# Scores and head mixing of an attention kernel as 64 by 64 products in the quarters of the TensorE array

## Chip, cores and metric

The kernel runs on one core of one Trainium2 chip. The metric is the time of one execution in microseconds (us), as the device measures it; of several runs the median counts. Engines are named as in the profile: PE is the matrix engine (TensorE) and PEld its weight loads, DVE the vector engine, ACT the scalar engine, POOL GpSimd, SP the engine that issues most of the transfers. A chunk is a set of rows of the score matrix that goes through the softmax together.

## What is computed

Talking-heads attention for 8 batches, 12 heads, 448 positions and head dimension 64, followed by a feed-forward layer with a squared ReLU:

```
scores = 0.125 * q @ k^T                      # per batch and head: 448 x 448
scores = einsum('bhij,hg->bgij', scores, w_pre)    # mixes the heads
attn   = softmax(scores, over j)
attn   = einsum('bhij,hg->bgij', attn, w_post)     # mixes the heads again
x      = (attn @ v), heads side by side       # 3584 x 768
out    = relu(x @ w_in)**2 @ w_out            # 768 -> 2048 -> 768
```

Inputs and output are float32; the products run in bfloat16.

## The kernel before, in words

**Scores.** A batch has 448 query rows: 384 of them in three sets r = 1, 2, 3 of 128 rows (row 3p + r - 1 of partition p), and 64 rest rows as set r = 0. `score` (L681) multiplies queries by keys. For r > 0 the contraction is 64 long, so the two heads of a pair go into the upper and lower half of the array's rows: two products 64x128 by 448 columns, each into its own PSUM bank, which run together. This is the planner's mode ROWS. DVE or ACT copies each bank into `snat` (L487, L489).

**Relayout and mixing.** Head mixing needs all heads of a row on different partitions. `relayout` has SP issue a transfer (L709) that gathers 10 rows times 12 heads from `snat` into the 120 partitions of one of 11 buffers `sch`, partition = row * 12 + head. `chunk` then multiplies by `wmix` (L807), a 120x120 matrix which holds ten copies of the 12x12 matrix `w_pre` on its diagonal, scaled and negated: one product 120x128 by 448 columns on the full array. A batch has 45 chunks: 6 of r = 0 (C0 = [0, 6, 19, 32]) and 13 of each other r, the first of which gathers leftovers. In the first batch 14 chunks take another way (L813), which the change leaves alone.

**Softmax and second mixing.** DVE reduces the bank to the minimum (L818), ACT takes the exponential with a running sum (L821), DVE the reciprocal (L827), POOL scales `wback`, the second mixing matrix, by it (L830). Four PE products (L837) multiply the exponentials by that matrix; this mixes, normalizes and transposes at once. The result is copied to `atb`. When half a batch is there, `av` (L882) multiplies by the values: two heads in the two halves of the array's columns, mode COLS.

**Feed-forward.** For every two batches `unit` runs `w_in` (L941), ReLU on DVE or ACT, the square on POOL (L962) and `w_out` (L980), on 128 or 256 columns at a time. These products have the lowest priority and fill PE's gaps.

**The order** is fixed when the kernel is built. `Planner.run` plays all operations through with a cost for each (a mix 190 ns, a pair's scores 190, a change of mode TURN = 95) and records them in the order in which they started; the engines then work strictly in that order. Each operation has a priority, in chunk numbers, and its inputs. PE prefers to stay in a mode, for at most STAY chunk numbers past an operation of another mode that is ahead. PSUM has 8 banks: MOST limits mixes ("m") to 3 banks, scores and others ("g") to 6, and the attention kinds together ("mix") to 7. Where PE would stand idle early in the run, `stand` (L1191) puts in products of zeros.

Of the kernel before, what the change touches and what calls it, by code (L numbers as in the profile page):

```python
# [23 lines left out]
NJ = 3  # L24
# [5 lines left out]
KC = CI * H  # L30
C0 = [0, 6, 19, 32]
# [15 lines left out]
ROWS, COLS = 1, 2  # L47
# [5 lines left out]
STAY = {ROWS: 2, COLS: 6}  # L53
# [4 lines left out]
MOST = {"m": 3, "a": 2, "f": 2, "g": 6, "mix": 7}  # L58
# [29 lines left out]
class Op:  # L88
    def __init__(self, engs, lat, pri, fn, deps, bank, frees, mode):
        self.engs, self.lat, self.pri, self.fn = engs, lat, pri, fn  # L90
        self.bank = bank if isinstance(bank, list) else [bank] if bank is not None else []
        self.frees, self.mode = frees, mode
        self.rows = None
        self.left, self.next, self.at, self.eng, self.ns = 0, [], None, None, 0
        for d in deps:
            if d is not None:
                self.left += 1
                d.next.append(self)
# [23 lines left out]
class Planner:  # L122
# [18 lines left out]
    def run(self):  # L141
# [22 lines left out]
        t, mode, clock = 0, 0, Clock()  # L164
# [16 lines left out]
        while True:  # L181
            for eng, heap in ready.items():
# [23 lines left out]
                kept, short, first = [], False, None  # L206
                while heap:
                    item = heapq.heappop(heap)
                    op = item[2]
                    if op.eng is not None:  # L210
                        continue
                    wide = len(op.bank) > 1
                    if not fits(op) or (short and op.bank and op.bank[0][0] in HOLD):
                        short = short or wide
                        kept.append(item)
                        continue
                    if eng == "PE" and mode and op.mode != mode and first is None:
                        first = item
                        kept.append(item)
                        continue  # L220
                    if first is not None:
                        if op.mode != mode or op.pri > first[0] + STAY[mode]:
                            kept.append(item)
                            if op.pri > first[0] + STAY[mode]:
                                op, item = first[2], first
                                kept.remove(first)
                            else:
                                continue
                    args = []
                    break  # L230
                else:
                    item = None
                    if first is not None:
                        kept.remove(first)
                        item, op, args = first, first[2], []
                if item is None and eng == "PE" and free and IDLE_FROM <= t < IDLE_END and (
                    t < 9000 or clock.at(t) > 1 or clock.share(t - SPELL, t) < IDLE_LOW
                ):
                    op = Op({"PE": 0}, 0, 0, self.still, [], None, None, mode)
                    op.eng, op.ns, op.at = "PE", IDLE_NS * clock.at(t), t  # L240
                    clock.spells.append((t, t + op.ns))
                    order.append((op, [free[0], mode]))
                    busy[eng] = t + op.ns
                    heapq.heappush(events, (t + op.ns, n, None))
                    n += 1
                if item is not None:
# [7 lines left out]
                    op.eng, op.ns, op.at = eng, op.engs[eng], t  # L254
                    if eng == "PE":
                        op.ns = (op.ns + TURN * (op.mode != mode)) * clock.at(t)
                        clock.spells.append((t, t + op.ns))
                        mode = op.mode
# [45 lines left out]
def kernel(  # L304
# [30 lines left out]
    sch = many(NSCH, "sch", [KC, S], BF16)  # L335
    schl = sb.tile([KC, S], BF16, name="schl")
    es = many(NE, "es", [KC, S], BF16)
    mn = many(NE, "mn", [KC, 1], F32)
    sm = many(NE // 2, "sm", [KC, 2], F32)
    rc = many(NE // 2, "rc", [KC, 2], F32)  # L340
    wq = many(NE, "wq", [KC, H, CI], BF16)
# [49 lines left out]
    wpre_rep = sb.tile([KC, H], F32, name="wpre_rep")  # L391
    wpost_rep = sb.tile([KC, H], F32, name="wpost_rep")
    smask = sb.tile([KC, CI], F32, name="smask")
    wmix = many(3, "wmix", [KC, P], BF16)
    for t_ in wmix:
        nc.vector.memset(t_[:, KC:P], 0.0)
    wback = sb.tile([KC, H, CI], F32, name="wback")
    nmask = sb.tile([KC, CI], F32, name="nmask")
    perm = sb.tile([KC, KC], BF16, name="perm")

    own = sb.tile([KC, H], F32, name="own")
# [14 lines left out]
    def pick(to, of, mask):  # L416
        parts = hr[0][0:KC, 0:H * H].rearrange("p (g h) -> p g h", g=H)
        nc.vector.tensor_tensor(
            out=parts, in0=wall[0:KC, H * H * of:H * H * (of + 1)].rearrange("p (h g) -> p g h", g=H),
            in1=mask[:, :].unsqueeze(1).to_broadcast([KC, H, H]), op=ALU.mult,  # L420
        )
        nc.vector.tensor_reduce(out=to[:, :], in_=parts, axis=AX.X, op=ALU.add)

    def pick_near():
        nc.vector.tensor_reduce(
            out=own[:, :], in_=ident[0:KC, 0:KC].rearrange("p (s h) -> p h s", s=CI), axis=AX.X, op=ALU.add,
        )
        pick(wpre_rep, 0, own)
        pick(wpost_rep, 1, own)
# [23 lines left out]
    def near_masks():  # L453
        nc.vector.tensor_reduce(
            out=smask[:, :], in_=ident[0:KC, 0:KC].rearrange("p (s h) -> p s h", s=CI), axis=AX.X, op=ALU.add,
# [5 lines left out]
            out=perm[:, :].rearrange("k (s x p) -> k s x p", s=CI, x=2),  # L461
            in_=ident[0:KC, 0:KC].rearrange("k (s p x) -> k s x p", s=CI, x=2),
        )

    def near_mix():
        for t_ in wmix[1:]:
            nc.vector.tensor_tensor(
                out=t_[:, 0:KC].rearrange("p (s h) -> p s h", s=CI),
                in0=wpre_rep[:, :].unsqueeze(1).to_broadcast([KC, CI, H]),
                in1=nmask[:, :].unsqueeze(2).to_broadcast([KC, CI, H]), op=ALU.mult,  # L470
            )

    def near_back():
        nc.gpsimd.tensor_tensor(
            out=wback[:, :, :], in0=wpost_rep[:, :].unsqueeze(2).to_broadcast([KC, H, CI]),
            in1=smask[:, :].unsqueeze(1).to_broadcast([KC, H, CI]), op=ALU.mult,
# [188 lines left out]
    def groups(b, r):  # L665
        size = GROUP if b >= GROUP_AT and r > 0 else 1
        return [range(p, p + size) for p in range(0, NPAIR, size)]

    def score(b, r, group):
        sn = store_of(b, r)  # L670
        p = group[0]
        tag = "g"
        keys = [(tag, "s", b, r, p_, x) for p_ in group for x in range(1 if r == 0 else 2)]

        def mms(*got):
            for key, slot in zip(keys, got):
# [4 lines left out]
                nc.tensor.matmul(slot[:, 0:S], lhsT=lhsT, rhs=kt[i][half, :, at_, :], start=True, stop=True)  # L681
# [7 lines left out]
            "PE", 190 * len(group), pri, keep(keys, mms), ins + old, lat=200, bank=keys, mode=ROWS * (r > 0),  # L689
        )  # L690
        for p_ in group:
# [23 lines left out]
    def relayout(b, c):  # L715
# [8 lines left out]
        if r == 2 and cc == 0:  # L724
            src_of[n] = schl
            here.append(move(n, pri, 780, deps + side.get(b - 1, []), schl[24:96, :], sn[120:126, :, :], lat))
# [13 lines left out]
        else:  # L740
            parts = [(blk, 0, KC, sn[cc - 1:cc + CPR * (CI - 1):CPR, :, :])]
        for of, r0, r1, srcs in parts:
            ns = 860 if r1 - r0 > 90 else 590
            relay_of.setdefault(of, []).append(move(n, pri, ns, deps + old, src_of[n][r0:r1, :], srcs, lat))
        if r == 0 and cc == 5 and b > 0:
            here.append(move(
                place_of(b, C0[2]), pri + 0.5, 500, deps + side.get(b - 1, []),
                schl[0:24, :], sn[124:P, 0:NPAIR, :], lat,
# [17 lines left out]

    def chunk(b, c):
        n = place_of(b, c)
        r, cc = block_of(c)
        rows = 96 if c == C0[2 if b else NJ] else KC  # L770
        ns = rows // H
        far = is_direct(b, c)
        src = None if far else src_of[n]
        wm = wmix[0 if r == 0 else 2 if cc == 0 and r < NJ else 1]
        back = wback_far if far else wback
# [50 lines left out]
        def f_rc():  # L826
            nc.vector.reciprocal(out=rc[i // 2][:, :], in_=sm[i // 2][:, :])  # L827
# [16 lines left out]
        def f_ac(eng):  # L844
# [6 lines left out]
        m = m_op[n] = add(  # L851
            "PE", mix_ns, n, keep(mk, f_m),
            relay.get(n, []) + [at_op.get(n - NE), w_ready if not far else None] + mix_deps, lat=200, bank=mk,
# [4 lines left out]
        e = exp_op[n] = add("ACT", 626, n + 0.4, f_exp, [x, at_op.get(n - NE), rc_op.get(n - NE)], lat=190, frees=mk)  # L858
        if n % 2 == 0:
# [5 lines left out]
        w = wq_op[n] = add("POOL", 370, n + 0.5, f_wq, [s_, at_op.get(n - NE)] + (backed_far if far else backed), lat=70)  # L865
# [147 lines left out]
    def pieces(pair, pos, part=None):  # L1013
        e0, e1 = (0, DMODEL) if part is None else part
        got = []
        for bb in range(2):
            row = (2 * pair + bb) * S
            for j, first in enumerate(PLACES[bb]):
# [9 lines left out]
                view = out[row:row + CPR * CI * NJ, :].rearrange("(s c r) e -> r c s e", c=CPR, r=NJ)  # L1028
# [24 lines left out]
    def w_turn(slot):  # L1053
        nc.tensor.matmul(
            slot[0:KC, 0:KC], lhsT=perm[:, :], rhs=wmix[1][:, 0:KC], start=True, stop=True,
        )

    def w_put():
        for t_, hi in ((wmix[0], KC), (wmix[2], 24)):
            nc.vector.tensor_copy(out=t_[0:hi, 0:KC], in_=slots["m", "w"][0:hi, 0:KC])  # L1060
# [6 lines left out]
    backed.append(add("POOL", 420, NEAR_AT, near_back, [fetched, masked]))  # L1067
    w_ready = add(
        "DVE", 300, NEAR_AT, w_put, [add("PE", 200, NEAR_AT, keep(("m", "w"), w_turn), [mixed], lat=200, bank=("m", "w"))], frees=("m", "w"),
    )  # L1070

# [74 lines left out]
    def next_batch(b):  # L1146
# [11 lines left out]
        for r in range(NJ + 1):  # L1158
            for p in groups(b, r):
                score(b, r, p)  # L1160
            for c in range(C0[r], (C0 + [NCHUNK])[r + 1]):
                relayout(b, c)
# [26 lines left out]
    def stand(slot, mode):  # L1189
        k_, m_ = P // 2 if mode == ROWS else P, P // 2 if mode == COLS else P  # L1190
# [41 lines left out]
```

## Time and profile before

| what | value |
|---|---|
| median of 3 runs | 579.14 us (579.02 to 579.38) |
| the profiled execution | 577.99 us |
| its span, first to last instruction | 576.2 us |
| granted PE clock, mean | 0.999 |
| mixes L807 on PE | 346 products (339 of `sch` recorded on one row, 7 of `schl` on another) |
| scores L681 on PE in row halves | 276 products |
| value transposes L837 | 1440 products |
| feed-forward L941, L980 | 1632 and 912 products |
| reduces L818, exponentials L821 | 360 each |

The table's counts are from the groups of the profile, which list source line, engine, operation, tiles, shapes and count, then the busy time and the mean duration of one, then the engine's idle time just before and what ended it. The mean duration of a PE product (354 ns for 448 columns) runs from its start to the end of its last column's way through the array. Products that follow each other overlap there, so the pace is read from start to start, on the timeline. "128*128" on a PE row are the rows and columns of the array that the product takes. The timeline gives start and length in us, and merges equal instructions that follow each other ("x4").

### The profile page before, as it was taken

How to read it: one execution, taken by the hardware profiler on the slowest of the kernel's cores; microseconds unless marked ns; L12 is line 12 of the kernel's file. 1: busy time of each engine (PE TensorE's matmuls, PEld its weight loads, DVE VectorE, ACT ScalarE, POOL GpSimd, SP SyncE). 2: the span in 40 equal slices, each digit the busy share in tenths (PEclk: the TensorE clock that was granted, in tenths of full speed). 3: DMA queues.
4: the chain of work that ended last, by engine and by line, in shares of the span. 5: the costliest groups of instructions: out<-in, count | busy, mean ns of one | idle time of the engine just before them, and what ended most of it. 6: DMA issues, size and time to landing. Idle time of an engine off the chain costs nothing.

```text
span 576.2 us, 16829 instructions
## 1 busy us (share of the span) xinstructions
PE 565.1 (98%) x5830; PEld 407.5 (71%) x5830; DVE 510.2 (89%) x1124; ACT 445.9 (77%) x1185; POOL 329.4 (57%) x609
## 2 busy tenths in 40 slices
PE   8999999999999999999999999999999999999997
PEld 5668766786776767677667677777758676767784
DVE  7999998999999999989899988999799898989442
ACT  5798988878778887988888988888888888888100
POOL 8267445764575548646567357845767444735341
PEclk9999999999999999999999999999999999999999
DMA  9999849963898639963697638984497646322021
GB/s 135 211 182 224 158 116 208 163 151 87 132 202 156 159 100 184 173 151 111 137 181 148 164 104 144 188 152 139 109 205 158 147 121 117 124 81 75 1 56 55
DMA packets 131678, 80.79 MB, mean 140 GB/s; under 512 B 59286, under 2 KB 126600, under 8 KB 131592
## 3 DMA queue, kind: packets, MB, share of 16 engines
q1 hardware_dynamic: 84760, 56.88, 40.3%
q0 software_dynamic: 46784, 22.81, 30.8%
q8 instruction: 45, 0.74, 0.6%
q14 instruction: 41, 0.34, 0.2%
q10 hardware_dynamic: 48, 0.02, 0.0%
HBM read 45.61 MB, written 11.01 MB: 98 GB/s over the span
## 4 chain that ended last, share of the span: by engine, by line
PE 87%; DVE 6%; DMA 3%; ACT 2%; issue 1%; POOL 0%; DVEq 0%; ACTq 0%; POOLq 0%
PE bank L980 24%; PE bank L941 23%; PE bank L837 12%; PE bank L807 11%; PE bank L882 7%; PE bank L681 6%; DMA sch<-snat 3%; PE bank L813 2%; DVE mn L818 1%; DVE atb L487 1%; DVE snat L487 1%; PE bank L1191 1%; ACT es L821 1%; DVE qn L612 1%; ACT snat L489 0%
## 5 line engine op out<-in xcount | busy, mean ns | idle before, releaser
L821 ACT ACTIVATE es<-bank,mn 120x448 bf16<-120x448 f32 x360 | 228.5, 643 | 37.0 <-DVE mn L818 32.6
L818 DVE TENSOR_REDUCE mn<-bank 120x1 f32<-120x448 f32 x360 | 209.7, 611 | 1.2 <-PE bank L807 1.1
L830 POOL TENSOR_SCALAR wq<-wback,rc 120x120 bf16<-120x120 f32 (+1 forms) x346 | 123.0, 367 | 148.4 <-DVE rc L827 90.3
L980 PE MATMUL bank<-w,h 128*128 128x384 bf16 (+2 forms) x912 | 184.1, 323 | 0.0
L941 PE MATMUL bank<-xt,w 128*128 128x256 bf16 (+1 forms) x1632 | 164.7, 254 | 0.3 <-ACT hr L959 0.2
L962 POOL TENSOR_TENSOR h<-hr 128x512 bf16<-128x512 f32 x112 | 116.4, 1041 | 64.8 <-DVE hr L955 34.9
L941 PEld LDWEIGHTS <-w 128*128 128x128 bf16 x1632 | 136.1, 98 | 22.8 <-issue 2.4
L837 PEld LDWEIGHTS <-es 120*112 120x112 bf16 (+1 forms) x1440 | 110.9, 129 | 27.7 <-ACT es L821 3.7
L837 PE MATMUL bank<-wq,es 120*112 120x120 bf16 (+1 forms) x1440 | 120.8, 217 | 0.5 <-ACT es L821 0.2
L980 PEld LDWEIGHTS <-h 128*128 128x128 bf16 x912 | 83.7, 98 | 51.7 <-issue 5.2
L487 DVE CAST atb<-bank 112x480 bf16<-112x480 f32 (+3 forms) x184 | 112.9, 622 | 7.8 <-PE bank L837 4.9
L489 ACT CAST atb<-bank 112x480 bf16<-112x480 f32 (+3 forms) x199 | 103.8, 537 | 19.1 <-PE bank L837 18.3
L807 PE MATMUL bank<-sch,wmix 120*128 120x448 bf16 (+1 forms) x339 | 108.2, 354 | 2.6 <-DVE snat L487 2.0
L487 DVE CAST snat<-bank 128x448 bf16<-128x448 f32 x153 | 89.1, 612 | 4.8 <-PE bank L681 2.7
L489 ACT CAST snat<-bank 128x448 bf16<-128x448 f32 x165 | 81.8, 546 | 7.7 <-PE bank L681 7.2
L821 ACT ACTIVATION_READ_ACCUMULATOR es<-bank,mn 120x1 f32 x360 | 75.1, 209 | 0.0
L955 DVE TENSOR_SCALAR hr<-bank 128x512 f32<-128x512 f32 x75 | 51.6, 688 | 19.3 <-PE bank L941 16.9
L807 PEld LDWEIGHTS <-wmix 120*128 120x128 bf16 (+1 forms) x346 | 31.2, 97 | 23.7 <-issue 10.9
L882 PE MATMUL bank<-atb,vs 112*64 112x192 bf16 (+3 forms) x864 | 40.4, 250 | 0.1
L681 PE MATMUL bank<-kt,qz 64*128 64x448 bf16 x276 | 39.7, 354 | 0.5 <-DVE snat L487 0.2
L882 PEld LDWEIGHTS <-vs 112*64 112x64 bf16 x864 | 36.5, 110 | 3.9 <-issue 2.4
L487 DVE COPY osb<-bank 128x384 f32<-128x384 f32 (+2 forms) x42 | 22.8, 543 | 16.8 <-PE bank L980 16.2
(72 smaller groups left out, 316.7 us busy)
## 6 DMA issues: line engine op xcount, KB each, us to landing
sch<-snat SPq DMA_DIRECT2D x318, 105.0 KB
out_dram<-osb SPq DMA_DIRECT2D x22, 360.0 KB
vs<-in_v_dram POOLq DMA_DIRECT2D x16, 336.0 KB, 8.4
ks<-in_k_dram POOLq DMA_DIRECT2D x14, 336.0 KB, 8.2
qs<-in_q_dram POOLq DMA_DIRECT2D x14, 288.0 KB, 9.1
w<-in_moe_w_in_dram POOLq DMA_DIRECT2D x6, 512.0 KB, 13.5
w<-in_moe_w_out_dram POOLq DMA_DIRECT2D x4, 768.0 KB, 21.4
out_dram<-osb SPq DMA_DIRECT2D x8, 192.0 KB
```

Of the source, the lines that this page charges most:

```text
L487: nc.vector.tensor_copy(out=out_, in_=in_)
L489: nc.scalar.copy(out=out_, in_=in_)
L681: nc.tensor.matmul(slot[:, 0:S], lhsT=lhsT, rhs=kt[i][half, :, at_, :], start=True, stop=True)
L807: nc.tensor.matmul(slot[:, 0:S], lhsT=wm[0:rows, :], rhs=src[0:rows, :], start=True, stop=True,)
L818: nc.vector.tensor_reduce(out=mn[i][0:rows, :], in_=slots[mk][0:rows, 0:S], axis=AX.X, op=ALU.min)
L821: nc.scalar.activation(out=es[i][0:rows, 0:S], in_=slots[mk][0:rows, 0:S], func=ACT.Exp, scale=-1.0, bias=mn[i][0:rows, 0:1], accum_out=sm ...
L830: nc.gpsimd.tensor_scalar(out=wq[i][0:rows, :, 0:ns], in0=back[0:rows, :, 0:ns], scalar1=rc[i // 2][0:rows, i % 2:i % 2 + 1], scalar2=1.0, ...
L837: nc.tensor.matmul(slot[0:P_KEYS, jb * H * ns:(jb + 1) * H * ns], lhsT=es[i][0:rows, jb * P_KEYS:(jb + 1) * P_KEYS], rhs=wq[i][0:rows, :, ...
L882: nc.tensor.matmul(v_[64 * hh:64 * hh + 64, i, 0:x1 - x0], lhsT=vs[:, 2 * c2 + hh, jb, :], rhs=atb[half][:, jb, 2 * c2 + hh, x0:x1], start ...
L941: nc.tensor.matmul(slot[:, j * w:(j + 1) * w], lhsT=w1[c2][:, (f0 + j) * 128:(f0 + j + 1) * 128], rhs=xt[:, c2, a:z], start=(c2 == 0), sto ...
L962: nc.gpsimd.tensor_tensor(out=h2_[:, f0:f0 + nf, 0:w], in0=hr[gi % 2][:, :].rearrange("p (f c) -> p f c", f=nf), in1=hr[gi % 2][:, :].rear ...
L980: nc.tensor.matmul(slot[:, 0:c1 - c0], lhsT=h2_[:, ft, mt * 128:(mt + 1) * 128], rhs=w2[:, ft, c0:c1], start=(ft == 0), stop=(ft == FT - 1),)
```

## The change

Five rows of a chunk take 60 partitions, and `wmix` holds nothing between different rows of a chunk. So of the 120x120 product only two blocks of 60x60 matter, and the other two quarters of the array are free for a second chunk. From the second batch on (PAIR_FROM = 1), `mix_two` mixes two chunks of a set r > 0 (all but the set's first chunk) with four 64x64 products; chunk data start at partition 4 (UP), so that rows 0 to 4 of a chunk lie on partitions 4 to 63 and rows 5 to 9 on 64 to 123.

- Row half x of source y goes to column half y of bank x. So each result bank holds half of the one chunk and half of the other. Chunk order, gather rows and output views are adapted; a second matrix `wback_two` puts the rows in order.
- `score` splits each product 64x128 of these batches into two 64x64. Four of them fill the quarters; a pair of heads still takes one pass of 448 columns. Score operations hold one pair where they held two (`groups`).
- Both kinds have the new mode BOTH. While PE is in another mode, the planner holds them until at least TOGETHER = 2 of them are ready and find banks (`company`), or until one is due: its priority is no more than MIX_DUE = 1.5 (SCORE_DUE = 1.0) past the newest chunk that has reached its exponential.
- Mixes may now hold 6 banks. The planner's costs are 205 ns for a score operation and 220 for a mix of two.
- At the start POOL clears partitions 0 to 3 of the 12 buffers (memsets), DVE clears the new edge columns of `wmix` and `perm`. Two of the zero fillers in `stand` (the 23rd and 29th) become 32 small quarter products each.

```diff
-ROWS, COLS = 1, 2
+ROWS, COLS, BOTH = 1, 2, 3
+PAIR_FROM, PAIRS, PAIR_MORE = 1, 1, 30
+UP, ZERO_AT = 4, 4
+TOGETHER, MIX_DUE, SCORE_DUE = 2, 1.5, 1.0
-STAY = {ROWS: 2, COLS: 6}
+STAY = {ROWS: 2, COLS: 6, BOTH: 8}
-MOST = {"m": 3, "a": 2, "f": 2, "g": 6, "mix": 7}
+MOST = {"m": 6, "a": 2, "f": 2, "g": 6, "mix": 7}
...
+        def company(heap):
+            f, left, got = len(free), dict(room), 0
+            for _, _, op in sorted(item for item in heap if item[2].mode == BOTH and item[2].eng is None):
+                kind, size = op.bank[0][0], len(op.bank)
+                if f >= size and left[kind] >= size and left["mix"] >= size:
+                    f -= size
+                    left[kind] -= size
+                    left["mix"] -= size
+                    got += 1
+            return got
...
+                alone = eng == "PE" and mode != BOTH and company(heap) < TOGETHER
...
+                    if alone and op.mode == BOTH and op.pri - front > op.due:
+                        kept.append(item)
                         continue
...
-        size = GROUP if b >= GROUP_AT and r > 0 else 1
+        size = 1 if b >= PAIR_FROM else GROUP if b >= GROUP_AT and r > 0 else 1
...
-                nc.tensor.matmul(slot[:, 0:S], lhsT=lhsT, rhs=kt[i][half, :, at_, :], start=True, stop=True)
+                for m0, m1 in ((0, P // 2), (P // 2, P)) if both else ((0, P),):
+                    nc.tensor.matmul(
+                        slot[m0:m1, 0:S], lhsT=lhsT[:, m0:m1], rhs=kt[i][half, :, at_, :], start=True, stop=True,
+                    )
...
+            if b >= PAIR_FROM:
+                o, pri = o // 2 + CPR // 2 * (o % 2), n - o % (2 * PAIRS) + 0.1 * (o % (2 * PAIRS)) - AHEAD
...
+    def mix_two(b, cs):
+        ns = [place_of(b, c) for c in cs]
+        keys = [("m", n) for n in ns]
+        srcs = [src_of[n] for n in ns]
+        w = wmix[1]
+
+        def mms(*got):
+            for i in range(0, len(got), 2):
+                for y in range(2):
+                    for x in range(2):
+                        k0, k1 = (64, KR) if x else (0, 64)
+                        o0, o1 = (64, KR) if y else (0, 64)
+                        c0 = (64 if y else 60) if x else (UP if y else 0)
+                        nc.tensor.matmul(
+                            got[i + x][o0:o1, 0:S], lhsT=w[k0:k1, c0:c0 + o1 - o0], rhs=srcs[i + y][k0:k1, :],
+                            start=True, stop=True,
+                        )
+
+        op = add(
+            "PE", 190 * len(cs) // 2 + PAIR_MORE, ns[0], keep(keys, mms),
+            [x for n in ns for x in relay[n]] + [w_ready], lat=200, bank=keys, mode=BOTH,
+        )
...
+        zeroed[id(t_)] = add("POOL", 470, ZERO_AT + 0.7 * i, lambda t_=t_: nc.gpsimd.memset(t_[0:UP, :], 0.0), [started])
```

## The prediction, before any run of the changed kernel

> **What bounds the kernel now.** I read the page's totals and the chain of work that ended last first, to learn which engine sets the end; then the groups that the change touches; then the PE timeline around them, start by start; then the waits and busy sums of the long middle stretch.
>
> ```profile
> PE 565.1 (98%) x5830; PEld 407.5 (71%) x5830; DVE 510.2 (89%) x1124; ACT 445.9 (77%) x1185; POOL 329.4 (57%) x609
> ...
> PE 87%; DVE 6%; DMA 3%; ACT 2%; issue 1%; POOL 0%; DVEq 0%; ACTq 0%; POOLq 0%
> ...
> L818 DVE TENSOR_REDUCE mn<-bank 120x1 f32<-120x448 f32 x360 | 209.7, 611 | 1.2 <-PE bank L807 1.1
> ...
> L807 PE MATMUL bank<-sch,wmix 120*128 120x448 bf16 (+1 forms) x339 | 108.2, 354 | 2.6 <-DVE snat L487 2.0
> ...
> L681 PE MATMUL bank<-kt,qz 64*128 64x448 bf16 x276 | 39.7, 354 | 0.5 <-DVE snat L487 0.2
> ```
>
> The chain runs 87% through PE. A busy PE need not be at its peak, so I set each start-to-start step in PE's records against its streaming time: 190 ns for 448 columns, 162 for 384, 109 for 256, 52 for 120, half of that where two products share the array, and 95 ns for each turn of the array's form (below). Over the run that makes 551.1 us; PE's records are 20.0 us longer, 12.1 of them before 100 us and only 7.9 in all the rest. The waits of PE between 100 and 530 us, and the engines' busy sums there:
>
> ```profile
> PE bank L807 <- DVE snat L487: 1.1, 1, 1.1
> PE bank L807 <- DVE atb L487: 0.4, 1, 0.4
> PE bank L941 <- ACT hr L959: 0.2, 1, 0.2
> PE bank L681 <- DVE snat L487: 0.2, 1, 0.2
> ```
> ```profile
> 100.00:530.00 430.00, 427.85 (x4343) 309.38 (x4341) 400.44 (x858) 359.58 (x963) 255.64 (x482) 1.00 0.71 143
> ```
>
> PE, the first figure after the length, is idle for 2.15 us of 430: dense feed-forward work (L941, L980) fills every gap of attention. So a microsecond off PE's work is a microsecond off the end, as long as DVE (third figure, 400.4) keeps its 30 us of room.
>
> **What a turn and a shared pass cost.** PE's timeline:
>
> ```profile
> 407.85 0.54 PE L807 MATMUL bank<-sch,wmix 120*128 120x448 bf16 x2
> 408.33 0.55 PE L681 MATMUL bank<-kt,qz 64*128 64x448 bf16 x4
> 408.81 0.50 PE L980 MATMUL bank<-w,h 128*128 128x384 bf16 x2
> ...
> 410.95 0.49 PE L980 MATMUL bank<-w,h 128*128 128x384 bf16 x2
> 411.38 0.85 PE L882 MATMUL bank<-atb,vs 112*64 112x256 bf16 x12
> ```
>
> Two mixes (2 x 190 ns) start at 407.85 and the scores 0.48 us later: 0.10 us is the turn from the full array to two row halves. Four scores take 0.48 us to the next full product: two passes of 187 ns, and a turn back. The L980 pair (2 x 162) to L882 at +0.43 shows the same turn into two column halves. Over all visits the medians are 96 ns into row halves, 92 into column halves, 95 out of either. Inside a visit the second of two products starts 3 ns behind the first, so halves do run together; the second pair comes 196 ns after the first's last product in row halves (187 + 9), and in column halves about 25 ns late at every width, which I read as its weights loaded only after the turn.
>
> **The change, part by part.** The order of the two programs' PE instructions gives the counts.
> - Mixing. Full mixes fall from 346 to 94. The 252 that go cost 252 x 190 ns = 47.9 us. In their place stand 126 groups of four quarter products of 448 columns: 126 x 187 = 23.6. **-24.3 us.**
> - Scores. 252 products in row halves (126 pairs) become 504 in quarters (126 groups). A pass of 448 columns carries two heads either way: no change.
> - Turns. Before, those scores stood in 63 visits to row halves. Now the 252 groups stand in 133 visits to quarters: 35 with one group, 77 with two, 21 with three. So 70 more visits, 140 turns x 95 ns: **+13.3 us.** No quarter turn is in the trace; the halves' 92 to 96 bound it.
> - Starts. Three starts of 3 to 4 ns ahead of a group's last product instead of one: 252 x 10 ns less 126 x 3: **+2.1 us.**
> - The late second group, in 98 of the visits. Nearest are column halves (25 ns; 64 weight columns, as here) and row halves (9 ns). Four loads in a row at 25 each would be 100 ns. I take 25, the row with the same loads: 98 x 25 = 2.5, less 63 x 9 = 0.6: **+1.9 us** (+0.3 at 9 ns, +9.2 at 100).
> - DVE, ACT and POOL keep their 360 reduces, exponentials and weightings; 124 partitions instead of 120 do not lengthen a row's 448 elements. Copies change sides by a dozen (atb: DVE 184 to 197; osb: 42 to 30). SP keeps 353 moves into sch and 56 stores, only in another order.
> - Set-up. 12 small POOL memsets stand between 11 and 20 us, where POOL idles 4.9 us ahead of its first L830; by the 0.22 us of the memset of ident up to twice that, 3 to 5 us, so mostly covered. Uncovered, they delay batch one's chunks by 1 us at most. Four DVE memsets of 0.09 us lie in DVE's wait of 0.88 us for the weights.
> - Waits. A pair of mixes waits for two moves instead of one, and queued behind it on PE are the value transposes (L837) and all the filling products. Walking along both orders with the durations above, the least lead of a mix over its L837 is 3.4 to 4.6 us by batch before and 3.4 to 4.7 after, so the order leaves the chain reduce, exponential, weighting as much time as it had. I take no added stall; -2 to +5 us are its bounds (a quarter of the 7.9 gone; two thirds more).
>
> Sum: -24.3 + 13.3 + 2.1 + 1.9 = **-7.0 us.** The profiled execution took 577.99 us (span 576.2 and 1.8 around it): 571.0. The median of the runs is 1.15 above it: **572.1 us.** What bounds next is DVE: its 30 us of room in the middle shrinks to some 25, so it does not take over.
>
> **Rivals.**
> 1. Loads one behind another. The L837 products with loads of 112 columns follow each other in 52 ns, so such a load takes at most that. If 64 columns took 52 too and four queued up, a group would need 208 ns instead of 197: 252 x 11 = +2.8, 574.9 us. Against it:
>
> ```profile
> L882 PE MATMUL bank<-atb,vs 112*64 112x64 bf16 x48 | 0.9, 197 | 0.0
> ```
>
> 48 products with 48 loads of 64 columns in 0.9 us, 19 ns each: four make 76 ns, which hide under 187. Chance 0.08. By the Trainium skill, "TensorEngine Tiling (Array Packing)", Restrictions and Gotchas, splitting columns switches off the fast weight load, and by "TensorE: Matmul & The Clock Gate", LDWEIGHTS, a load takes its columns over 1.2 GHz, 53 ns for 64, so four in a row 213 ns; the sum by it would be 252 x 16 ns worse, an estimate of -3.0. The 19 ns above already speak against loads in a row.
>
> 2. Four do not go at once, only two. Rows alone and columns alone are in the trace, both together are not. Then a group takes 374 ns: +252 x 187 = 47 us, 619 us. Chance 0.03. The Trainium skill ("TensorE: Matmul & The Clock Gate", Measured speedup vs the span model) says that row and column splits compose and that a tile adds about 4 ns; nothing in the runs before shows it.
>
> 3. Slower: DVE paced in twos. A pair puts two chunks on L818 at once, two banks must be free together, and DVE is busy for 93% of the middle. Where its reduces or bank copies come late, PE stands in order before the next pair, and no filling product may pass. 126 pairs: from 55 ns of such waiting each, the 7.0 us are gone; at 100 ns (12.6 us) it is 584.7 us. For it: 93%, and one long wait of this kind already, 1.1 us for a snat copy. Against: the 30 us of room and the equal leads. Chance 0.10, 0.07 of it over the bound.
>
> 4. The gain is hidden: were the chunk's chain across engines what paces attention, PE's saving would become idle PE, 579 us. PE's 2.15 us of idle in 430 speak against it. Chance 0.05.
>
> 5. More: second groups 9 ns late and the lower bound of the stalls, -7.0 - 1.6 - 2 = -10.6, 568.5 us. Chance 0.08.
>
> That the planner does not bring groups together is ruled out by its order: 98 of 133 visits hold two or three.
>
> **How the numbers follow.** Forecast 0.66, rivals 0.08, 0.03, 0.10, 0.05, 0.08. I count as no change what lies within 0.2% (1.2 us), about what a measurement here can tell: 578.0 to 580.3. Faster: 0.66 + 0.08 + 0.08 = 0.82; same: 0.05 + 0.03 = 0.08; slower: 0.07 + 0.03 = 0.10. The forecast's own range with its bounds is 568.5 (-1.6 and -2) to 577.1 (+5). The range reaches down to 567.5 for rival 5 and up to 579 for rival 4 and the light part of 3; left out are rival 2 and most of 3.
>
> **What would show it.** On PE's timeline: a visit of two groups from start to the next full product in about 0.5 us (2 x 187 + 20 + 25 + 95), 133 visits, turns near 95 ns; quarter groups of 448 columns 187 to 210 ns apart. PE's idle between 100 and 530 us still near 2 us, DVE's share up by a point. Wrong would be a group of 220 ns or more, turns far over 95, a second group 100 ns late, or new PE waits on L818, L487 or the moves of some microseconds.

## The result

| | before | changed |
|---|---|---|
| median of 6 runs each | 579.08 us (578.17 to 579.38) | 584.14 us (580.96 to 585.69) |
| profiled execution | 577.99 us | 581.89 us |
| its span | 576.2 us | 580.1 us |

Changed to before: 1.008, 95% interval 1.0059 to 1.0102. The kernel became slower by some 0.8%, where 572.1 us and "faster" with 0.82 were forecast; 584.1 lies outside the range of 567.5 to 579.0. The runs also spread more. The profiled execution is 2.3 us faster than the changed kernel's median, so part of the loss stands in no trace.

The page of the changed kernel:

```profile
PE 563.6 (97%) x6390; PEld 399.3 (69%) x6390; DVE 503.3 (87%) x1125; ACT 452.9 (78%) x1192; POOL 333.0 (57%) x619
...
PE 86%; DMA 5%; DVE 3%; ACT 3%; issue 1%; POOL 0%; DVEq 0%; ACTq 0%; POOLq 0%
...
L885 DVE TENSOR_REDUCE mn<-bank 124x1 f32<-124x448 f32 (+1 forms) x360 | 208.9, 612 | 4.8 <-PE bank L820 4.0
...
L715 PE MATMUL bank<-kt,qz 64*64 64x448 bf16 (+1 forms) x528 | 46.2, 364 | 1.0 <-ACT qz L521 0.7
L820 PE MATMUL bank<-sch,wmix 64*64 64x448 bf16 x504 | 43.4, 362 | 2.0 <-DMA sch<-snat 1.8
```

Nothing here looks alarming. DVE's reduces did not get longer, PE is still busy for 97%, and the chain still runs through PE for 86%. But the share of transfers on the chain went from 3% to 5%. The sums of 100 to 530 us show a little more idle PE (5.2 us instead of 2.15), and DVE with more room, not less:

```profile
100.00:530.00 430.00, 424.77 (x4819) 300.18 (x4817) 391.99 (x857) 365.28 (x965) 254.37 (x479) 1.00 0.75 146
```

So I took PE's records apart as in the prediction: the streaming times and turns; what each step took beyond them, split at 60 ns into lateness and stalls; and what follows the last product's start.

| us | before | changed | forecast of the difference |
|---|---|---|---|
| streaming and turns, by order | 551.1 | 540.7 | -11.0 |
| lateness up to 60 ns, before / after 100 us | 1.3 / 4.2 | 3.8 / 7.8 | +4.0 in all |
| stalls over 60 ns before 100 us | 9.3 | 11.2 | 0 |
| stalls over 60 ns after 100 us | 3.6 | 8.9 | 0 |
| from the last product's start to the end | 4.1 | 5.4 | 0 |

The differences add to -10.4 + 6.1 + 1.9 + 5.3 + 1.3 = +4.2; the span grew by 3.9. The rows leave out 2.6 and 2.3 us of the two spans; for the kernel before they hold 18.4 us beyond the 551.1, where the prediction had 20.0.

**The quarters do what was forecast.** A visit with two groups on PE's timeline:

```profile
464.54 1.47 PE L1049 MATMUL bank<-w,h 128*128 128x384 bf16 x8
465.93 0.57 PE L820 MATMUL bank<-sch,wmix 64*64 64x448 bf16 x8
466.43 0.63 PE L905 MATMUL bank<-wq,es 124*112 124x120 bf16 x8
```

From 465.93 to the next product 0.50 us pass, as the prediction wrote down. The records show a turn into quarters at 93 ns, starts 3 ns apart, the second group 213 ns after the first (187 + 26), a third one 189 ns after the second, and 283 ns from the last start of a visit of two to the next full product (187 + 96); all are medians.

**The waits are new.** PE in two places, and DVE at the first of them:

```profile
67.89 0.35 PE L874 MATMUL bank<-sch,wmix 124*128 124x448 bf16 x1
70.70 0.35 PE L874 MATMUL bank<-sch,wmix 124*128 124x448 bf16 x1 [2.46 <-DVE snat L519]
70.89 2.71 PE L1010 MATMUL bank<-xt,w 128*128 128x128 bf16 x24
...
261.40 0.57 PE L820 MATMUL bank<-sch,wmix 64*64 64x448 bf16 x8
263.32 0.38 PE L820 MATMUL bank<-sch,wmix 64*64 64x448 bf16 x2 [1.35 <-DMA sch<-snat]
264.13 0.38 PE L820 MATMUL bank<-sch,wmix 64*60 64x448 bf16 x2 [0.44 <-DMA sch<-snat]
```
```profile
66.80 0.41 DVE L519 CAST xt<-bank 128x256 bf16<-128x256 f32 x1
70.03 0.62 DVE L519 CAST snat<-bank 128x448 bf16<-128x448 f32 x1 [2.82 <-DMA sch<-snat]
```

At 67.9 us PE waits for a bank that DVE has to empty into `snat`, and DVE waits for a transfer that still reads `snat`. The granted clock then drops to 0.5 for 3.4 us (70.95 to 74.36): 24 products that take 56 ns elsewhere need 2.7 us, 110 each. At 261 us PE stands inside a visit because the third pair's two transfers have not landed; the planner had put three pairs in a row, and nothing may pass.

### The profile page after: what moved, and what is told of

The parts are those of the page before. It is cut to its first block, busy times and chain, and to the rows that moved or that the text cites. A ratio compares the mean times of both kernels' runs of the same rounds, so it can differ in the third digit from the quotient of the medians.

```text
span 580.1 us, 18046 instructions
## 1 busy us (share of the span) xinstructions
PE 563.6 (97%) x6390; PEld 399.3 (69%) x6390; DVE 503.3 (87%) x1125; ACT 452.9 (78%) x1192; POOL 333.0 (57%) x619
## 4 chain that ended last, share of the span: by engine, by line
PE 86%; DMA 5%; DVE 3%; ACT 3%; issue 1%; POOL 0%; DVEq 0%; ACTq 0%; POOLq 0%
PE bank L1010 25%; PE bank L1049 24%; PE bank L905 13%; PE bank L715 6%; PE bank L951 6%; PE bank L820 5%; DMA sch<-snat 3%; PE bank L874 3%; PE bank L880 2%; ACT es L888 2%; DMA kt<-kn 2%; PE bank L1286 1%; DVE atb L519 1%; PE bank L581 1%; DVE mn L885 1%
## 5 line engine op out<-in xcount | busy, mean ns | idle before, releaser
L888 ACT ACTIVATE es<-bank,mn 124x448 bf16<-124x448 f32 (+1 forms) x360 | 229.1, 644 | 30.3 <-DVE mn L885 26.8
L885 DVE TENSOR_REDUCE mn<-bank 124x1 f32<-124x448 f32 (+1 forms) x360 | 208.9, 612 | 4.8 <-PE bank L820 4.0
L898 POOL TENSOR_SCALAR wq<-wback_two,rc 124x120 bf16<-124x120 f32 x252 | 89.6, 368 | 81.8 <-DVE rc L895 58.2
L905 PEld LDWEIGHTS <-es 124*112 124x112 bf16 (+2 forms) x1440 | 107.0, 129 | 28.9 <-issue 6.2
L519 DVE CAST atb<-bank 112x480 bf16<-112x480 f32 (+2 forms) x197 | 118.0, 609 | 7.9 <-PE bank L905 6.4
L905 PE MATMUL bank<-wq,es 124*112 124x120 bf16 (+2 forms) x1440 | 118.9, 217 | 1.5 <-ACT es L888 0.6
L521 ACT CAST atb<-bank 112x480 bf16<-112x480 f32 (+2 forms) x186 | 99.3, 545 | 25.7 <-PE bank L905 24.8
L888 ACT ACTIVATION_READ_ACCUMULATOR es<-bank,mn 124x1 f32 (+1 forms) x360 | 75.2, 209 | 0.0
L715 PE MATMUL bank<-kt,qz 64*64 64x448 bf16 (+1 forms) x528 | 46.2, 364 | 1.0 <-ACT qz L521 0.7
L820 PE MATMUL bank<-sch,wmix 64*64 64x448 bf16 x504 | 43.4, 362 | 2.0 <-DMA sch<-snat 1.8
```

The lines of the kernel that those rows point to most:

```text
L519: nc.vector.tensor_copy(out=out_, in_=in_)
L521: nc.scalar.copy(out=out_, in_=in_)
L715: nc.tensor.matmul(slot[m0:m1, 0:S], lhsT=lhsT[:, m0:m1], rhs=kt[i][half, :, at_, :], start=True, stop=True,)
L820: nc.tensor.matmul(got[i + x][o0:o1, 0:S], lhsT=w[k0:k1, c0:c0 + o1 - o0], rhs=srcs[i + y][k0:k1, :], start=True, stop=True,)
L885: nc.vector.tensor_reduce(out=mn[i][0:rows, :], in_=slots[mk][0:rows, 0:S], axis=AX.X, op=ALU.min)
L888: nc.scalar.activation(out=es[i][0:rows, 0:S], in_=slots[mk][0:rows, 0:S], func=ACT.Exp, scale=-1.0, bias=mn[i][0:rows, 0:1], accum_out=sm ...
```

## The experiments

Theory A: PE waits in its fixed order for late transfers. Theory B: the loss lies in the first 75 us. Theory C: the quarters cost more than reckoned; the trace already spoke against it. The later runs came from what A and B left open. All medians are of 6 to 12 runs; the kernel before ran beside each.

**1 and 2. Both kernels without the chunk transfers.**

```diff
-        op = add("SP", ns, pri, lambda: nc.sync.dma_start(out=outs, in_=srcs), deps, lat=680)
+        op = add("SP", ns, pri, lambda: None if n >= NCHUNK and not lat else nc.sync.dma_start(out=outs, in_=srcs), deps, lat=680)
```

> The kernel before with the transfers into the chunk buffers (L709 into sch) left out from batch two on, so that mixes read what the first batch left there; the planner still reckons with them, so the order on every other engine is the same. It leaves out the relayout, the rest is computed. Theory A (the changed kernel lost its 7 us to PE waiting in its fixed order, above all for the transfers of a pair): the kernel before has some 3 us of such waits after 95 us (1.1, 1.3, 0.6 us ahead of L807), so about 576 us. Theory B (the loss lies in the first 75 us and in the clock that drops there): the same, as it is only the baseline for the next run.

> The changed kernel with the same transfers left out, PE order unchanged. Theory A: the waits of L820 for transfers go (2.7 us over 0.1 us each in the profile) and what was late behind them too; about 7 us below the run of the kernel before without transfers, 568 to 573 us, and little spread between runs. Theory B: the 2.6 us stall at 68 us and the clock drop behind it may stay where they do not hang on a transfer; then 577 to 580. Theory C (the quarter passes or turns cost more than the sum said): 580 or more, no better than with transfers.

Measured: 576.75 us for the kernel before (0.998 of the kernel beside it, 1.2 us less) and 575.88 for the changed one (0.9969 where it had 1.008, 6.4 us less). Transfers, with what they set off, hold some 5 us of the loss; the spread shrank from 4.7 to 2.9 us. Stalls after 100 us fell from 8.9 to 4.4 us, and those ahead of a mix from 3.2 to 0.1. But the lead is 0.9 us and not 7, so A is not all. My reading of the waits of the kernel before was wrong as well: its 3.6 us of stalls stayed without transfers. The wait at 68 us stays, since the first batch's transfers do:

```profile
PE bank L874 <- DVE snat L519: 3.2, 1, 3.2
```

**3 and 4. Pairing never, and from the third batch on** (PAIR_FROM = 8 and 2).

> The changed file with pairing from batch 9 on, that is never: the shift by four partitions, the memsets and the two quartered fillers stay, scores and mixes run as before. Theories A and C: within 1 us of the kernel before, 578 to 580. Theory B in the form that set-up or fillers cost: 581 to 584.

> Pairing from the third batch on instead of the second. By products and turns it has 3 us more work on PE than the changed kernel. Theory B: the early stall and clock drop go, 3 to 5 us, so 579 to 582. Theory A: waits are spread over all batches, so 583 to 587, slower by the 3 us less gain or about equal to the changed kernel.

Measured: 581.24 us (1.005, 1.0033 to 1.0068) and 581.7 (1.0089, 1.0054 to 1.0124). Without a single pair the file is 3 us slower than the kernel before. Its operations stand in another order, and stalls after 100 us are 6.2 us instead of 3.6. That was not expected. Besides the shift, the memsets and the fillers, the limit of 6 banks for mixes stays in this file; no run changes one of these alone. From the third batch on, the early stall and clock drop are gone (8.1 us of stalls before 100 us), yet 9.1 us stand after it. B alone falls.

**5. From the third batch on, without transfers.**

> Pairing from the third batch on, and the chunk transfers of batch two on left out as before (the planner still reckons with them). The stall at 68 us, where copies into snat wait for transfers of the first batch, is not in this order. If what is left against the kernel before without transfers (576.75 us) is the forecast's work term alone, six sevenths of -7.0: -6.0 or some 571 us, and more with other stalls. Theory C (quarter visits cost what the sum did not reckon): 575 or more.

Measured: 576.61 us, where 571 was expected, no better than the kernel before without transfers. Its table named what was missing: streaming and turns are 7.4 us less than before, lateness 4.1 more, stalls after 100 us 1.5 more (before it some 0.6 less), and the end 1.7 us longer (5.5 instead of 3.7). The 571 was also set too low: with the 3 us of more work that run 4 reckoned for pairing from the third batch on, the work term is -4, not -6. The longer end stood in the profile of the changed kernel too; it has nothing to do with PE, and led to run 12.

**6 to 8. Transfers earlier, or reckoned later** (AHEAD = 9; 1500 instead of 500 ns to landing in `move`).

> The changed kernel with AHEAD = 9 instead of 7: a transfer may stand two chunk numbers earlier in SP's queue, and scores move up with it. Its PE work is the same within 1 us. Theory A (PE waits for pairs' transfers): fewer such waits, 576 to 580 us, less spread. Theory A' (transfers cannot go earlier, as they wait for one of the 11 buffers or behind SP's transposes): no change, 582 to 585.

> The changed kernel where the planner reckons 1.5 us instead of 0.5 us from the end of a chunk transfer to the mix that may start, from batch two on. Mixes stand later in PE's order, behind filling products, and PE waits less for transfers. Work on PE +0.3 us. Theory A: 576 to 581 us. If the waits come from elsewhere: 583 to 586.

> The same edit in the kernel before, as a control. Its waits for transfers are some 3 us in all; up to 2 us may go: 576 to 579. If any other order costs a few us, as in the run with pairing never, 580 to 582: then the order of the kernel before is a lucky one and part of the loss is no matter of quarters.

Measured: 597.14, 582.97 and 578.25 us. Letting transfers stand earlier in SP's queue made it far worse: 20.7 us of stalls after 100 us. SP works in order, and I take it that an early transfer that waits for its buffer holds up all behind it; no run shows that by itself. Reckoning a later landing did next to nothing. Both expectations of A failed: more room in the plan is not what lacks. The control stayed at the kernel before.

**9 to 11. Fourteen buffers instead of eleven** (NSCH = 14; the start-up rows moved into h2 to make room).

> The changed kernel with 14 chunk buffers instead of 11 (room comes from placing the small start-up rows inside h2, which is unused then). A pair keeps two buffers until both are mixed together, so transfers wait longer for a free one. Theory A (late transfers, because buffers come free late): the lead from a transfer's issue to its mix grows back, waits fall, 575 to 580 us. Theory A' (transfers late for other reasons, queue order on SP and contention with loads): 582 to 586.

> The control, 14 buffers in the kernel before: its waits for transfers are some 3 us, so 576 to 579 us under either theory; 580 to 582 if any other order than its own is worse.

> Pairing from the third batch on, with 14 buffers. Work on PE by products and turns 7 us less than before, with starts and late groups some 3.5 us less; the ends' 1.3 us (below) stay. Theory A: 575 to 578 us, a gain over the kernel before. Theory A': 580 to 582, as with 11.

Measured: 579.76 us for the changed kernel (1.0013, 1.0001 to 1.0025), 582.22 for the kernel before (1.0054, 1.0035 to 1.0073), 579.67 from the third batch on (1.0011, 0.9992 to 1.0029). Against the kernel before beside each run, three buffers give the changed kernel 3.9 us back and cost the other 3. But they also change the plan: from the 17th product on, PE's order is another one. In the profile of run 9 the stall at 68 us and the slow clock behind it are gone, and PE's waits for `sch` between 100 and 530 us fall from 1.8 to 0.2 us. Yet stalls after 100 us are still some 9 us; they now stand mostly before scores (L716) and value transposes (L906):

```profile
PE bank L716 <- DVE atb L520: 1.0, 1, 1.0
```

The time from a transfer's issue to its mix, with transfers and mixes matched in their order after 100 us, moved as theory A says. One in ten was below 8.1 us before, below 5.9 in the changed kernel, and below 8.0 with 14 buffers. It does not show that pairs shorten it: one in ten was below 4.9 us in run 3, which has no pair, and below 9.9 in run 10, which is 3 us slower than the kernel before. That a pair, which holds two buffers until both can be mixed, needs a longer ring stays an argument.

**12. The store view alone, in the kernel before.**

```diff
-                view = out[row:row + CPR * CI * NJ, :].rearrange("(s c r) e -> r c s e", c=CPR, r=NJ)
+                view = out[row:row + CPR * CI * NJ, :].rearrange("(s c r) e -> r c s e", c=CPR // 2 if 2 * pair + bb >= 1 else CPR, r=NJ)
```

> The kernel before with only the output view of the change: rows stored as 6 groups of 20 instead of 12 of 10 (this permutes output rows; nothing else changes, and the order on PE, DVE, ACT and POOL is the same). In the changed kernel's profile the last packet ended 3.8 us after the last product's start instead of 2.5. Theory: the store's outer count sets how many DMA engines share it, so +1.3 us at the end: 579.2 to 579.5 against 578. If the tail had another cause: no change.

Measured: 581.3 us, 1.0038 (1.0026 to 1.005), +2.3 us, with nothing changed on PE, DVE, ACT or POOL. 1.3 us of it is the end (4.1 to 5.4); stalls after 100 us rise by 1.2. From the first to the last packet a store of 120 rows took 2.0 us (median) as 12 groups of 10, and 3.1 us as 6 groups of 20. The transfers at the end of both kernels (columns: length, busy engines, clock, DMA share, GB/s), before and changed:

```profile
573.10:574.60 1.50, 0.00 (x0) 0.00 (x0) 0.00 (x0) 0.00 (x0) 0.00 (x0) 0.97 0.44 126
```
```profile
575.70:576.70 1.00, 0.00 (x0) 0.00 (x0) 0.00 (x0) 0.00 (x0) 0.00 (x0) 1.00 0.37 112
576.70:578.50 1.80, 0.00 (x0) 0.00 (x0) 0.00 (x0) 0.00 (x0) 0.00 (x0) 1.00 0.26 80
```

No engine computes there: the last stores move at 126 GB/s with 0.44 of the DMA engines before, and at 112, then 80 GB/s with 0.37, then 0.26 in the changed kernel. The trace even counts the engines. Each engine that takes part in a transfer ends it with a packet of 4 bytes; in the last microseconds, with four stores of 120 rows and four of 8, there are 80 such packets before, 56 in the changed kernel and 92 in run 15 below: 4 x 8 and 4 x 12, 4 x 6 and 4 x 15. The Trainium skill states this rule: by "DMA: Bandwidth & Descriptors", Why a DMA increments its semaphore by 16 and not by 1, a transfer runs on the largest number up to 16 that divides the slowest dimension of both its sides, so 12, 6 and (for 120) 15. The trace agrees. It was the page to weigh in the prediction, and I did not.

**13 and 14. The old view in the changed kernel, without transfers and with 14 buffers.**

> The changed kernel without the chunk transfers from batch two on, and with the output view of before (12 groups of 10; output rows are permuted). PE order unchanged. If store view, transfers and the forecast's work term add up: 575.9 - 2.3 = 573.6 us, 3 us below the kernel before without transfers (576.75); what then lacks to -7 is the stall at 68 us with the slow clock behind it (some 4 us in the profile). If the store view costs only through transfers: 575 to 576.

> The changed kernel with 14 chunk buffers and the output view of before (output rows permuted), PE order as with 14 buffers. If buffers and store view are separate causes: 579.8 - 2.3 = 577.5 us, below the kernel before by 1.5. If they are one cause (stores and transfers collide): 579 to 580.

Measured: 575.37 us (0.9937, 0.992 to 0.9954) and 578.37 (0.9998, 0.9987 to 1.0009). Against the kernel before without transfers (0.998) the first is 0.4% or some 2.5 us faster. Its profiled span is 571.1 against 575.4 us, 4.4 less, but that execution is the fastest of its six. Before 100 us, where the early stall and the slow clock behind it stand, PE loses some 2 us more in it than in run 1. With these 2 us added, 4.5 us of the forecast's 7 are there by the medians and 6.4 by the profiles; the rest stays open. Against the kernel before, the old view gave 0.9 us with 14 buffers (1.0013 to 0.9998), where it gave 1.9 without transfers (0.9969 to 0.9937). So store view and transfers are not two causes that simply add; why not, no run shows.

**15 and 16. A store in one run of 120 rows, with 11 and with 14 buffers.**

```diff
-            o = cc - 1
+            o, d = cc - 1, CPR
             if b >= PAIR_FROM:
-                o, pri = o // 2 + CPR // 2 * (o % 2), n - o % (2 * PAIRS) + 0.1 * (o % (2 * PAIRS)) - AHEAD
-            parts = [(blk, 0, KC, sn[o:o + 1 + CPR * (CI - 1):CPR, :, :])]
+                d, pri = 2, n - o % (2 * PAIRS) + 0.1 * (o % (2 * PAIRS)) - AHEAD
+            f = 20 * (o // 2) + o % 2 if d == 2 else o
+            parts = [(blk, 0, KC, sn[f:f + 1 + d * (CI - 1):d, :, :])]
...
-                    "(s c r) e -> r c s e", c=CPR // 2 if 2 * pair + bb >= PAIR_FROM else CPR, r=NJ,
+                    "(s c r) e -> r c s e", c=1 if 2 * pair + bb >= PAIR_FROM else CPR, r=NJ,
```

> The changed kernel with other rows paired: the sources of a pair are every second of 20 neighbouring rows, so each mixed chunk holds 10 rows in a row and a block's 120 rows are stored in one run of 120. The computation is the reference's; the orders of all engines are unchanged. Theory of the store view: a long outer count spreads over more DMA engines than 6, so the 2.3 us come back, 581 to 582.5 against 584. If gathering from 20 neighbouring partitions is slower than from every twelfth: 585 and more.

> Both repairs: linear store and 14 buffers. If both causes are what they seem, 577 to 578 us, faster than the kernel before by 1 to 2; if the gather suffers, 581 or more.

Measured: 577.75 us (0.9988, 0.9965 to 1.0012; the runs spread from 574.6 to 582.3) and 577.06 (0.9978, 0.9964 to 0.9992). With orders of all engines unchanged, the other rows brought the changed kernel from 1.008 to 0.9988. The end is 3.4 us; a store takes 1.8 us from first to last packet, and its issue on SP 0.46 us (median; 0.33 at the least) where 12 groups took 0.83 (0.77 at the least). Of the 3.5 us by which the profiled span is shorter than the changed kernel's, 2.0 are the end; stalls after 100 us are still some 9 us. The run also gathers from every second partition instead of every twelfth, so its gain is not the store's alone. With 14 buffers as well, pairing beats the kernel before by some 0.2%:

```profile
PE 86%; DVE 6%; ACT 2%; DMA 2%; issue 2%; POOL 0%; DVEq 0%; ACTq 0%; SPq 0%; POOLq 0%
```

DMA is back from 5% to 2% of the chain; in run 15 it is still 5%, in run 9 it is 4%. Some 9 us of stalls after 100 us remain here too.

**17 and 18. The linear store in the kernel before, and 14 buffers with pairing from the third batch on.**

> The control for the linear store: the kernel before, from batch two on, with chunks of 10 neighbouring rows, so that 120 rows are stored in one run; it computes the reference, the orders are unchanged. If the gain of the repaired kernels is the quarters', this is within 1 us of the kernel before. If a linear store is what gains (an issue on SP takes 0.33 us instead of 0.77), 576 to 577.5. If gathering from 10 neighbouring partitions is slow: 580 and more.

> Linear store and 14 buffers, pairing from the third batch on, so that the second batch, where transfers collide with the loads of the weights, stays in its old form. Work on PE 2 to 3 us more than with pairing from the second batch. 575 to 577 if fewer waits pay for that, 578 to 580 if not.

Measured: 602.59 us (1.042) and 578.04 (0.998, 0.9969 to 0.9992). Run 17 is no clean control: to store in one run, it gathers from 10 neighbouring partitions, and transfers get slow; DMA is 9% of its chain:

```profile
PE 78%; DMA 9%; DVE 6%; ACT 2%; issue 1%; SPq 1%; POOL 1%; ACTq 0%; DVEq 0%; POOLq 0%
```

So how much of run 16's lead a faster store would give the kernel before stays open. Run 18 is no better than 16. In its profile stalls after 100 us are only some 4 us, but before it there are some 13, where run 16 has some 10, and PE has 2.4 us more work: leaving the second batch as it was moves the loss and does not remove it.

## Why the prediction was wrong

- **Bound, turns, quarters: right.** PE stayed the bound, four products go at once, a turn costs 93 to 96 ns. Streaming, turns and lateness give -10.4 + 6.1 = -4.3 us against -7.0. Of the lateness 2.5 us fall before 100 us, 1.2 of them in the slow clock behind the stall at 68 us; without these 2.5 it is -6.8.
- **The first step that failed: "SP keeps 353 moves into sch and 56 stores, only in another order."** I counted the transfers and did not look at their shapes, though the diff shows the view from 12 to 6 groups. The stores became half again as long: +1.3 us at the end, which no work hides, +2.3 us in all where nothing else was changed (run 12), and with the orders kept some 5 us between the changed kernel and run 15, which also gathers other rows.
- **The second and larger one: "I take no added stall", with +5 as its bound.** It was 7.2 us in the profile, of the 11.2 us between forecast and profile: 1.9 before 100 us and 5.3 after it. Runs 1 and 2 show on what the 5.3 hang: without the chunk transfers the two kernels differ there by 0.8 us (4.4 against 3.6). I compared the lead of a mix over its L837, which indeed did not shrink, and not that of a transfer over its mix. Why the transfers come late is shown in part. The stores' shape is one cause (+1.2 us of stalls in run 12, without a pair, 1.0 of it one stall before scores). 14 buffers took 3.9 us off, but with another order on PE, and some 9 us of stalls after 100 us remain, so what the buffers do by themselves is not shown.
- **Rival 3, slower through DVE paced in twos**, had the side right and the cause wrong; that its 584.7 us lies close to the 584.1 measured is luck. PE does stand before pairs with nothing passing, but the transfers were late; DVE's room grew.
- **Open:** runs 3 and 10 show that orders other than the planned one of before can cost 3 us without any pair (in run 10 one stall of 3.0 us at 118 us, with the slow clock behind it), while run 8 costs nothing. A rival that no run tests is the limit of 6 banks for mixes: it stays in run 3, where one lead in ten of a transfer over its mix is below 4.9 us with no pair at all. How much of the changed kernel's waits belongs to pairs, and how much to a plan that fits less well by chance, the runs don't separate.
- **The Trainium skill's pages in the prediction.** That row and column splits compose (the Trainium skill, "TensorE: Matmul & The Clock Gate", Measured speedup vs the span model) the trace now shows, with 3 ns from start to start. Four loads of 53 ns in a row (rival 1) it does not show: a third group follows after 189 ns, not 213.

## What to carry to other kernels

When a change permutes rows, price every transfer whose shape it alters, first those behind the last computation, where nothing hides them. When two operands are consumed together, ask how long each now holds its buffer, and measure the lead from issue to use. And a term of PE work that comes out nearly right says little about the time while PE waits in a fixed order: look at who can be late.

## What the runs showed of the hardware

- The same 120 rows stored as 12 groups of 10, 6 groups of 20 or one run of 120 took 2.0, 3.1 and 1.8 us from first to last packet, and 0.83, 0.77 and 0.46 us to issue on SP (medians).
- Gathering ten rows of 12 heads from every twelfth partition, every second, and neighbouring ones, an 896-byte packet took 48, 58 and 64 ns (mean, 300 to 420 us), and for neighbours one in ten over 118. With neighbours, and the store in one run, the kernel lost 4%. By the Trainium skill, "SBUF — State Buffer", Door 1, four neighbouring partitions share a DMA port; ten neighbours then reach three ports, an estimate from its table. That fits, and no run here separates it from other causes.
- A stall of PE of 2.6 us was followed by 3.4 us at half the granted clock. The eleven other stalls of 2.2 to 4.7 us in the traces of the runs came with 3.4 or 6.8 us at half clock as well, begun during the stall or within 1.3 us after it; one of 1.9 us (run 17) did not.
